# Fewer steps with a third product, and a weight's narrowing moved between two sums, in an FNet and gated-convolution kernel

## The chip, the cores and the metric

The kernel runs on one core of one Trainium2 chip. A core has TensorE (PE, the matrix engine; the profile lists its weight loads apart, as PEld), VectorE (DVE), ScalarE (ACT), GpSimd (POOL) and SyncE (SP), each with a queue of its own that runs in order. They meet through semaphores, on-chip memory (SBUF) and the eight banks of PSUM, into which TensorE writes. The metric is the time of the whole program on the device, in microseconds (us).

## The reference

Two layers follow each other. The first takes the real part of a Fourier transform over the sequence and the features; the second is a feed-forward layer whose gate is a convolution of length three over the sequence:

```python
# x: (8, 3136, 256) float32
x = np.fft.fft(np.fft.fft(x, axis=1), axis=2).real
h = np.maximum(x @ w_in, 0.0)                    # w_in: (256, 1024)
hp = np.pad(h, ((0, 0), (1, 1), (0, 0)))
conv = sum(conv_w[k] * hp[:, k:k + 3136] for k in range(3))   # conv_w: (3, 1024)
out = (h * (1.0 / (1.0 + np.exp(-conv)))) @ w_out             # w_out: (1024, 256)
```

All of it is float32. The weights `w_in`, `conv_w` and `w_out` come in as float64 and are read as pairs of 32-bit words.

## The kernel before

**Transform over the sequence.** For each batch the input is folded (`fold_ops`: 14 VectorE operations or pairs of them, about 1.2 us each) and then multiplied with tables of cosines and sines on TensorE, in nine "units" for the first batch and eight for the others. A unit has matmuls into a PSUM bank, for some a ScalarE copy, and a `fin`, two VectorE operations that write sums and differences. The results are two tables for a batch, `PQ[b][0]` (named `pt`) and `PQ[b][1]` (named `qt`), the cosine part and the sine part. The units for even frequencies k are `even_even` and `even`, those for odd k `odd_even` and `odd`. They use the symmetry of the transform: the frequencies k and S - k share both parts and differ only in the sign of one.

**Second layer.** The transform over the features is multiplied into `w_in` beforehand (`blocks`, `column`, giving `G` and `ge`). The main loop has 256 steps: 8 batches, 4 chunks of frequencies, 8 blocks of 128 hidden features. Step s passes through a pipeline of four cycles. In cycle t of the loop:

- `products(t + 1)`: on TensorE, `pb` is G1 times `qt`, and `pa` (seeded beforehand by ScalarE) gets G0 times `pt` added. The hidden values are relu(pa + pb) for the front rows and relu(pa - pb) for the mirrored back rows.
- `copies(t + 1)`: ScalarE copies `pb` into SBUF (`nb`), once with scale 1 for the front and once with scale -1 for the back.
- `combine(t)`: VectorE makes the two halves of `h`, each by a saturating add of `pa` and `nb` (L719).
- `seed(t + 2)` and `first_tap(t)` on ScalarE, `tap(t - 1, 1)` and `tap(t - 1, 2)` on VectorE (L730): the convolution, into `g`.
- `sigmoid(t - 2)` on ScalarE, `gate(t - 2)`: the product with `h`, shared between GpSimd (L753) and VectorE (L754).
- `mm2(t - 3)`: TensorE multiplies `g` into `w_out`, six or seven output tiles, summed over eight steps.

Side work is hung onto cycles in a table `side`, under (cycle, place): places are "first", "act", "dve", "pool", "load" and "pe". The folds of the next batch but one go to "dve", the units' matmuls of the next batch to "pe", their copies to "act" and their `fin` to "dve". VectorE's place "dve" lies between the two taps.

**The third product.** In some steps (`triple(s)`, which asks `third(i)`) TensorE adds G1 times `qt` to `pa` as well. Then `pa` holds the front half whole, ScalarE writes its relu (L705) instead of the copy for the front, and scales the copy for the back by -2 (L703). VectorE has one add less in `combine`. In the same cycles the gate is shared otherwise (`shares`): GpSimd takes a quarter of the columns instead of half, VectorE three quarters. `third(i)` holds for steps from 3 to `ends[2]` (44) that have side work in "dve" and none in "pe".

**The start.** A weight is made float32 by integer operations on its 32-bit words (`narrow`): a first part `power` (L543, L547, L548) and a second part `product` (L551, L557, L558, L561), seven VectorE operations for a quarter of `w_in`. `Weight.parts` returns the two as functions; `Weight.narrow` runs both at once. Near the end of the start, the units `us[4], us[2], us[3], us[7], us[8]` run in this order: the unit of the middle feature (its `fin` on GpSimd), then `even_even(1)`, `even(1)`, `even_even(0)`, `even(0)`. The second quarter, `w_in[1]`, is narrowed ahead of them (L821). It is used by `column(1)` and `blocks(1)` later. After the units come `column(0)` and `blocks(0)`, which take their PSUM banks from the same pool of four (`spare`) as the units.

Of the kernel before, what the change touches and what calls it, by code (L numbers as in the profile page):

```python
# [36 lines left out]
def kernel(  # L37
# [199 lines left out]
    def mend_row(par, half):  # L237

        for st in range(2):
            row = tabs[par][96:NP, st, HQ - 1]  # L240
            act(row, row, AF.Copy, scale=half[96:NP])
# [239 lines left out]
    def spread(b, cs):  # L481

        for c in cs:
            ch = chunks[c]
            eb[b, c] = ebp.tile([P, HN], F32, name="eb", tag="eb")[:, 0:ch.k1 - ch.k0]
            nc.sync.dma_start(out=eb[b, c], in_=ed[b:b + 1, ch.k0:ch.k1].to_broadcast([P, ch.k1 - ch.k0]))
# [121 lines left out]
    def raw_in(i):  # L608
        def f(sh):
            if i % 2 == 0:  # L610
                raws[i // 2] = wp.tile([P, 2, *sh[1:]], I32, name="raw", tag="w%d" % (i // 2))
            return raws[i // 2][:, i % 2]
        return f

    w_in = [Weight(w4[i], moe_w_in[:, i * N4:(i + 1) * N4].rearrange("(t p) n -> p t n", p=P), raw_in(i))
            for i in range(4)]
# [57 lines left out]
    def triple(s):  # L674

        return third(steps.index(s))

    def third(i):

        return 3 <= i < ends[2] and (i, "dve") in side and (i, "pe") not in side  # L680

    def row_of(s):
        hs[s] = hp.tile([P, HW], F32, name="h", tag="h")
# [48 lines left out]
    def shares(s):  # L732


        ch = chunks[s[1]]
        w = ch.w - 2
        n = ch.rest[0] if ch.last else w
        m = n - n // (4 if third(steps.index(s) + 2) else 2)
        return slice(0, m), slice(m, n), slice(n, w)
# [78 lines left out]
                                   lambda sh: xp.tile(sh, I32, name="raw", tag="xh"))  # L818
                    w_out.load(nc.sync)
    mend_row(0, half)  # L820
    w_in[1].narrow(0, 2)  # L821
    for i, u in enumerate(us[j] for j in (4, 2, 3, 7, 8)):
        u.matmuls(0, 1)
        u.copy()
        u.fin()
        if i == 0:
            flip()
            store()
            spread(0, range(1, len(chunks)))
# [13 lines left out]
    side = {}  # L843
# [23 lines left out]
    ends = [9, 20, per + 12] + [per * (b - 1) - 3 + max(11 - 4 * (b - 2), 0) for b in range(3, B)]  # L867
# [163 lines left out]
```

## Time and profile before

| | |
|---|---|
| time, median of 3 runs | 1192.77 us (1191.79 to 1192.78) |
| span of the profiled execution | 1191.0 us |
| TensorE busy | 1166.1 us (98%) |
| VectorE busy | 1128.6 us (95%) |
| ScalarE busy | 888.2 us (75%) |
| GpSimd busy | 408.9 us (34%) |
| records of pa<-qt, the third product | 44, 18.0 us |

A float32 product of the program appears as two matmul records, so the 44 records are 22 products. Matmuls are pipelined: the distance from one start to the next is what a matmul costs, and it is less than its record's length. The same holds for VectorE, where an operation's record (0.55 us for an add) is a little longer than the distance to the next (0.47 us). In an order of time each line shows the start, the length, the engine, the line of the code, the operation, what it writes and reads, and how many are merged; a bracket gives the idle time ahead of it and what ended it. L92 is the line of the helper that issues all matmuls.

### The profile page before, as it was taken

What the parts mean: (1) busy time and instruction counts of PE and PEld (TensorE: products, weight loads), DVE (VectorE), ACT (ScalarE), POOL (GpSimd) and SP (SyncE); (2) the same over time, 40 slices, a digit from 0 to 9 for tenths busy, and PEclk for the clock granted to TensorE, in tenths of its full rate; (3) what the DMA queues carried; (4) which work ended last, traced back from release to release, by engine and by line L of the source; (5) the groups of instructions that cost most, each with busy time, mean ns of one, the idle gap of its engine ahead of it and who ended that gap; (6) DMA issues with size and microseconds to landing.
All of it is one profiled execution on the core that took longest, in us unless ns stands there. A gap on an engine that the chain in (4) does not pass through costs nothing.

```text
span 1191.0 us, 15384 instructions
## 1 busy us (share of the span) xinstructions
PE 1166.1 (98%) x4846; PEld 897.9 (75%) x4846; DVE 1128.6 (95%) x1620; ACT 888.2 (75%) x1888; POOL 408.9 (34%) x476
## 2 busy tenths in 40 slices
PE   4999999999999999999999999999999999999998
PEld 2667777777777777777777777777777777777776
DVE  7899999899999999999998999999998998999996
ACT  2578667777678777877777777877786777888885
POOL 5226343423334333333333243432322232222222
PEclk9899999999999999999999999999999999999999
DMA  9803233121122121202121010310010100110001
GB/s 229 191 8 110 53 57 88 49 62 47 40 69 79 34 72 57 63 26 74 34 88 52 28 54 27 102 34 27 27 34 21 32 28 27 47 34 27 28 27 31
DMA packets 70068, 66.08 MB, mean 55 GB/s; under 512 B 28107, under 2 KB 57683, under 8 KB 69987
## 3 DMA queue, kind: packets, MB, share of 16 engines
q1 hardware_dynamic: 64349, 51.98, 15.6%
q0 software_dynamic: 5120, 12.85, 3.7%
q8 instruction: 38, 0.62, 0.2%
q14 instruction: 43, 0.35, 0.1%
q10 hardware_dynamic: 518, 0.28, 0.1%
HBM read 39.33 MB, written 25.74 MB: 55 GB/s over the span
## 4 chain that ended last, share of the span: by engine, by line
PE 93%; DVE 3%; ACT 1%; POOL 1%; issue 1%; DMA 0%; SPq 0%; POOLq 0%; ACTq 0%; DVEq 0%
PE po L92 56%; PE pa L92 15%; PE pb L92 14%; PE pd L92 8%; DVE g L730 1%; POOL xh L131 1%; DVE g L754 0%; DVE h L719 0%; DVE wout L551 0%; ACT os L778 0%; DVE raw L558 0%; ACT nb L708 0%; ACT g L725 0%; DMA out_dram<-os 0%; DVE wout L561 0%
## 5 line engine op out<-in xcount | busy, mean ns | idle before, releaser
L92 PE MATMUL po<-wout,g 128*128 128x256 f32 x3072 | 705.2, 379 | 2.7 <-DVE g L754 2.7
L92 PEld LDWEIGHTS po<-wout,g 128*128 128x128 f32 x3072 | 581.5, 189 | 144.7 <-issue 19.7
L730 DVE SCALAR_TENSOR_TENSOR g<-h,cw,g 128x770 f32<-128x770 f32 (+1 forms) x512 | 576.6, 1126 | 7.5 <-ACT g L725 3.9
L753 POOL TENSOR_TENSOR g<-g,h 128x385 f32<-128x385 f32 (+3 forms) x256 | 273.0, 1067 | 717.5 <-ACT g L745 555.7
L708 ACT ACTIVATE nb<-pb 128x386 f32<-128x386 f32 (+2 forms) x468 | 208.6, 500 | 172.5 <-PE pb L92 171.7
L745 ACT ACTIVATE g<-g 128x385 f32<-128x385 f32 (+5 forms) x512 | 244.6, 531 | 67.6 <-DVE g L730 64.2
L719 DVE CUSTOM_DVE_ANT_0 h<-pa,nb 128x386 f32<-128x386 f32 (+3 forms) x490 | 253.9, 556 | 6.4 <-POOL h L686 4.2
L725 ACT ACTIVATE g<-h,cw 128x770 f32<-128x770 f32 (+1 forms) x256 | 244.0, 953 | 0.0
L92 PE MATMUL pb<-qt,G 127*128 127x387 f32 (+2 forms) x512 | 214.3, 499 | 0.9 <-ACT G L641 0.9
L92 PE MATMUL pa<-pt,G 128*128 128x387 f32 (+2 forms) x512 | 211.8, 494 | 0.0
L672 ACT ACTIVATE pa<-eb,ge 128x387 f32<-128x387 f32 (+2 forms) x256 | 155.1, 606 | 0.6 <-ACT ft L477 0.6
L92 PEld LDWEIGHTS pa<-pt,G 128*128 128x128 f32 x512 | 97.1, 190 | 73.8 <-issue 18.4
L754 DVE TENSOR_TENSOR g<-g,h 128x385 f32<-128x385 f32 (+3 forms) x256 | 150.3, 587 | 2.4 <-ACT g L745 2.4
L92 PE MATMUL pd<-tab,w 98*128 98x196 f32 (+3 forms) x448 | 115.9, 356 | 0.0
L92 PEld LDWEIGHTS pb<-qt,G 127*128 127x128 f32 x512 | 91.7, 191 | 18.9 <-ACT G L641 2.0
L131 POOL DMA_INDIRECT xh<-in_x_dram,idx x64 | 99.7, 1558 | 13.0 <-issue 10.5
L92 PEld LDWEIGHTS pd<-tab,w 98*128 98x128 f32 (+1 forms) x448 | 82.7, 191 | 12.6
L778 ACT COPY os<-po 128x256 f32<-128x256 f32 x196 | 57.6, 396 | 6.6 <-PE po L92 3.3
L156 DVE TENSOR_TENSOR xh<-xh 98x1020 f32<-98x1020 f32 (+1 forms) x32 | 40.7, 1276 | 2.6 <-DMA xh<-in_x_dram,idx 2.5
L167 DVE TENSOR_TENSOR xh<-xh 98x1024 f32<-98x1024 f32 (+1 forms) x32 | 40.5, 1267 | 0.1
L178 POOL COPY w<-xh 98x4 f32<-98x4 f32 (+1 forms) x32 | 22.9, 716 | 6.1 <-DVE xh L167 3.6
L193 DVE TENSOR_TENSOR w<-xh 98x508 f32<-98x508 f32 (+1 forms) x32 | 23.5, 733 | 0.1
(124 smaller groups left out, 359.5 us busy)
## 6 DMA issues: line engine op xcount, KB each, us to landing
out_dram<-os SPq DMA_DIRECT2D x192, 128.0 KB
xh<-in_x_dram SPq DMA_DIRECT2D x16, 784.0 KB
eb<-ed SPq DMA_DIRECT2D x16, 193.5 KB
tab<-dft_seq_dram SPq DMA_DIRECT2D x4, 589.5 KB
raw<-in_moe_w_in_dram SPq DMA_DIRECT2D x4, 512.0 KB
raw<-in_moe_w_out_dram SPq DMA_DIRECT2D x1, 2048.0 KB
eb<-ed SPq DMA_DIRECT2D x8, 209.0 KB
eb<-ed SPq DMA_DIRECT2D x7, 193.0 KB
```

The source lines that it names most:

```text
L92: nc.tensor.matmul(o, l, r, start=start, stop=stop, skip_group_check=True)
L131: nc.gpsimd.indirect_dma_start(out=xh[b, h][0:NP, 7 - m].rearrange("p q d -> p (q d)"), out_offset=None, in_=bass.AP(tensor=x.tensor, offs ...
L156: vt(a[:, :, :, 1:D], a[:, :, :, 1:D], r[:, :, :, D - 1:0:-1], op=ALU.add)
L672: act(pa[s][:, 0:n], eb[b, c], AF.Copy, scale=ge[:, f:f + 1])
L708: act(nb[s][:, i, cols], p[:, cols], AF.Copy, scale=-1.0 if i else 1.0)
L719: nc.vector._custom_dve(TENSOR_ADD_SAT, out=to, in0=a[:, cols], in1=c[:, i, cols], s0=BIG, s1=0.0)
L725: act(gs[s], hs[s][:, 0:n], AF.Copy, scale=cw[:, 0, s[2]:s[2] + 1])
L730: stt(out=g, in0=h[:, k:k + n], scalar=cw[:, k, f:f + 1], in1=g, op0=ALU.mult, op1=ALU.add)
L745: act(gs[s][:, c], gs[s][:, c], AF.Sigmoid)
L753: gt(g[:, p], g[:, p], h[:, p], op=ALU.mult)
L754: vt(g[:, v], g[:, v], h[:, v], op=ALU.mult)
L778: nc.scalar.copy(out=osb[:, j % 2], in_=pt[:, j % 2])
```

## The change

There are two edits, and neither changes what is computed.

```diff
     def third(i):
-        return 3 <= i < ends[2] and (i, "dve") in side and (i, "pe") not in side
+        return 3 <= i < 12 and (i, "dve") in side
```

The third product is kept in steps 3 to 11 only. It relieves VectorE at the price of TensorE; the edit is meant to give TensorE its time back in the steps after 11.

```diff
     mend_row(0, half)
-    w_in[1].narrow(0, 2)
+
+    second = w_in[1].parts(0, 2)
     for i, u in enumerate(us[j] for j in (4, 2, 3, 7, 8)):
         u.matmuls(0, 1)
         u.copy()
+        for f in second[i - 1:i]:
+            f()
         u.fin()
         if i == 0:
             flip()
```

The slice is empty for i = 0, holds `power` for i = 1 and `product` for i = 2, and is empty again after that. So `power` now runs on VectorE ahead of the `fin` of `even_even(1)`, and `product` behind it and ahead of the `fin` of `even(1)`. It is meant to let VectorE finish the first of these sums earlier.

## The prediction

> **What bounds the kernel now.** I read the chain of waits first, then the stretches of the middle of the run, then the orders of time of TensorE and VectorE there, then those of the start.
>
> ```profile
> PE 93%; DVE 3%; ACT 1%; POOL 1%; issue 1%; DMA 0%; SPq 0%; POOLq 0%; ACTq 0%; DVEq 0%
> ```
> The chain of what ended last is 93% TensorE (PE), so in most of the run each microsecond of matmul is a microsecond of span. The busy shares (PE 98%, VectorE (DVE) 95%) warn that VectorE is close behind. By stretch (columns: length; busy of PE, weight load, DVE, ACT, POOL; granted clock; DMA):
> ```profile
> 107.00:120.00 13.00, 13.00 (x57) 9.79 (x56) 12.84 (x18) 10.69 (x31) 7.92 (x7) 1.00 0.36 105
> 185.00:257.00 72.00, 72.00 (x295) 53.78 (x294) 66.78 (x90) 54.12 (x115) 24.91 (x34) 1.00 0.18 54
> 257.00:330.00 73.00, 73.00 (x310) 56.59 (x309) 71.03 (x106) 52.73 (x112) 28.33 (x26) 1.00 0.19 58
> ```
> 107 to 140 us holds steps 12 to 17, 185 to 257 us steps 29 to 43. PE never idles there; VectorE has 5.2 us left of 72. Two cycles of PE, the first with the third product (pa<-qt), the second without:
> ```profile
> 236.51 0.81 PE L92 MATMUL pb<-qt,G 127*128 127x387 f32 x2
> 237.16 0.81 PE L92 MATMUL pa<-pt,G 128*128 128x387 f32 x2
> 237.81 0.82 PE L92 MATMUL pa<-qt,G 127*128 127x387 f32 x2
> 238.47 2.75 PE L92 MATMUL po<-wout,g 128*128 128x256 f32 x12
> 241.06 0.82 PE L92 MATMUL pb<-qt,G 127*128 127x387 f32 x2
> 241.71 0.82 PE L92 MATMUL pa<-pt,G 128*128 128x387 f32 x2
> 242.37 2.75 PE L92 MATMUL po<-wout,g 128*128 128x256 f32 x12
> ```
> From start to start, a product takes 0.65 us (237.81 to 238.47), a cycle 4.55 us with the third and 3.90 us without. VectorE's cycle of step 40, which has the third product:
> ```profile
> 240.62 0.55 DVE L719 CUSTOM_DVE_ANT_0 h<-pa,nb 128x386 f32<-128x386 f32 x1
> 241.09 1.13 DVE L730 SCALAR_TENSOR_TENSOR g<-h,cw,g 128x770 f32<-128x770 f32 x1
> 242.14 0.68 DVE L171 TENSOR_TENSOR xh<-xh 99x512 f32<-99x512 f32 x1
> 242.74 0.68 DVE L172 TENSOR_TENSOR xh<-xh 99x512 f32<-99x512 f32 x1
> 243.34 1.01 DVE L730 SCALAR_TENSOR_TENSOR g<-h,cw,g 128x770 f32<-128x770 f32 x1
> 244.28 0.75 DVE L754 TENSOR_TENSOR g<-g,h 128x578 f32<-128x578 f32 x1
> 245.19 1.03 DVE L719 CUSTOM_DVE_ANT_0 h<-pa,nb 128x386 f32<-128x386 f32 x2 [0.17 <-DVE g L754]
> ```
> One saturating add, two taps of 0.93, a fold of 1.2 us, a gate of 0.67: 4.4 us against PE's 4.55. Without the third product it will be two adds and a smaller gate against 3.90: VectorE becomes the longer of the two in every such step. That is the question of this change.
>
> The start, where the second edit lies (VectorE, then PE):
> ```profile
> 39.74 0.69 DVE L561 SCALAR_TENSOR_TENSOR win<-raw,win 128x512 f32<-128x512 f32 x1
> 40.35 0.35 DVE L298 TENSOR_TENSOR as<-as,po 128x197 f32<-128x197 f32 x1
> 40.62 0.35 DVE L300 TENSOR_TENSOR as<-po,as 128x196 f32<-128x196 f32 x1
> ```
> ```profile
> 41.07 1.67 PE L92 MATMUL po<-dm,win 128*128 128x1 f32 x8 [0.82 <-ACT eb L835]
> ```
> The narrowing (seven operations from 35.44 us, ending with L561) stands ahead of the sums L298 and L300, although their input was copied by ScalarE at 37.37. L300 releases the PSUM bank that column(0) takes, and PE idles 0.82 us until 41.07; the view names a ScalarE copy done at 40.78, but L300, ending at 40.97, fits better.
>
> **What the Trainium skill says.** "SBUF — State Buffer", section "SBUF: two separate sides": VectorE operations with two SBUF inputs and GpSimd operations that read SBUF contend for one port pair, held for a whole instruction. The trace agrees: the tap's shortest record is 1.00 us, and the one that meets a GpSimd gate at 257.73 takes 1.48. "GPSIMD Engine Reference", section "4.1 Engine selection": two-input elementwise work is about twice as slow on GpSimd; here 385 columns take 0.87 us against VectorE's 0.55. "TensorE: Matmul & The Clock Gate", section "What's actually happening": the array runs at half clock after an idle window of about 3.4 us and needs a busy one to return. Here the granted clock is 0.99 in 37.9 to 41.3 us, 0.50 in 41.3 to 48.1, and 1.00 after, which fits two such windows.
>
> **First edit: which steps.** A step has the third product now if it is in 3 to 43, has VectorE side work and no PE side work. By the schedule in the code these are 3 to 13, 15, 17, 29, 30, 32, 34, 35, 37, 38, 40 and 42: 22 steps, which matches the 44 records of pa<-qt. After the change 3 to 11 remain. All nine have it already, so dropping the PE condition changes nothing. Thirteen steps lose it.
>
> Per step lost: **PE** -0.65 us (-0.71 for the 418 columns of steps 29 and 30). **ScalarE** two copies before, two after (L703 and L705 0.49 each, L708 0.50 each): nothing. **VectorE** +0.47 for the second add (start to start: two take 0.94, one 0.47); the gate falls from three quarters to half of 770 columns, 0.67 to 0.47, so -0.20; net +0.27. **GpSimd** gate 192 to 385 columns, 0.52 to 0.87 us, +0.35, hidden as such (busy 25 of 72 us), but it can block VectorE. Bounds of that block: 0 (the operations don't meet) and 0.35 a step (all exposed). The tap means of the stretches, 1.076 us where nine of sixteen steps have the quarter share and 1.087 where none has, nearly coincide, so I take 0.05.
>
> The output products of step s wait for VectorE's gate of s, which ends where its adds of step s+3 begin. Hence a ledger of both engines.
>
> Steps 12 to 18, VectorE in one piece from 107.08: its cycles 4.19, 4.70, 4.50, 4.0, 4.42, 4.19, 4.41 become, with +0.27 in 12, 13, 15 and 17, ends of 111.5, 116.5, 121.0, 125.3, 129.7, 134.2, 138.6. PE, 0.65 less in four cycles, would reach its output products earlier than these ends allow and waits 0.4, 0.6 and 1.1 us in cycles 12 to 14. Of 2.6 us saved 0.75 are left at cycle 18. With the contention I take **0.5**. VectorE is then 0.9 us late, but steps 19 to 28 carry matmuls of the next batch on PE (46 us of PE against 44 of VectorE without its waits), so it catches up and the 0.5 stays.
>
> Steps 28 to 42: VectorE takes from 184.70 to 253.12, 68.42 us, of which 5.07 idle by its brackets (0.89, 0.17, 0.20, 0.25, 0.45, 0.92, 1.76, 0.26, 0.17), so 63.35 of work; +9 x 0.32 gives 66.2. PE goes from 185.07 to 253.41, 68.34; less 7 x 0.65 and 2 x 0.71 it is 62.4. VectorE now sets the pace. Its end becomes 184.70 - 0.5 + 66.2 = 250.4, which is when the output products of cycle 43 can start, instead of 254.72: **4.3 earlier**, with the first 0.5 inside it. PE alone could have been there at 248.2. Its lead of 2.5 us over the need at step 28 is used up, so cycle 44, where VectorE takes 4.87 us (257.00 to 261.87) and PE 4.56, costs **0.3** back. After that PE has longer cycles (5.2 us) and the old state returns. Sum: -4.0.
>
> **Second edit.** The two halves of the narrowing (three and four operations) move behind the first and second unit of even k. No operation is added. The three end at 37.05, the sums wait for ScalarE's copy (37.37), end near 38.0; then the four (3.3 us before, partly stretched by GpSimd work up to 39.16, say 3.0) end near 41.1 and the second unit's sums near 42.1, as before. So nothing behind is delayed. Column(0) follows the matmul that ends at 40.25 without a gap, 0.8 earlier, and ends about 41.75. Blocks(0), which began at 42.55 behind it, then waits for the second unit's sums (42.1) and starts **0.4 to 0.5 earlier**; PE, ScalarE and then VectorE (idle 0.90 before its first adds) follow, so it carries through. I take -0.5.
>
> Together: 1192.8 - 4.0 - 0.5 = **1188.3**.
>
> **Rivals.**
> (1) VectorE binds in place of PE, as worked out: 1188.3. For it: 5.2 us of VectorE slack in 72, and its work a step. Chance 0.58.
> (2) The same, and the closed gap keeps the clock up: blocks(0) take 3.76 us at half clock, the same matmuls 1.89 at 51.03. With some of the next products about 2.2 saved: 1186.1. Against it: PE soon waits again for the second unit's sums. Chance 0.13.
> (3) VectorE's waits absorb everything and PE gets its full 11 x 0.65 + 2 x 0.71 = 8.6: 1183.7. Against it: the 66.2 above. Chance 0.05.
> (4) The whole 0.35 of longer GpSimd work lands on VectorE: 9 x 0.3 more is 2.7 in the second stretch, and the first gains nothing: about 1191.3. For it: the 1.48 us tap. Chance 0.16.
> (5) Slower: each larger GpSimd gate blocks VectorE for its whole 0.87 us. The second stretch then is 63.35 + 9 x 1.14 = 73.6, 5.2 above today, less the lead of 2.5, so +2.7; the first has no gain: about 1195.5. Against it: today's half-share steps lose about 0.07 us a tap. Chance 0.08.
>
> **How the numbers follow.** The forecast is (1). The range from 1185.6 to 1191.5 takes in (1), (2) and (4), 0.87 less some spread at its ends. The bound of 0.2% is 2.4 us, so faster is below 1190.4: (1) to (3) and a quarter of (4), 0.80; within the bound the rest of (4), 0.12; slower (5), 0.08.
>
> **What would show it.** Right: pa<-qt has 18 records and the adds 503; PE shows idle time released by VectorE's gate (L754) of about 2 us in steps 12 to 14 and about 2 in 28 to 45; VectorE loses its 5 us of idle time there; column(0) starts near 40.3. Wrong: PE without idle time (rival 3), taps clearly longer than 1.09 us (4, 5), or waits of VectorE for GpSimd's memsets or ScalarE's copies in 29 to 42, which I count as gone.

## The result, and the profile after

The changed kernel takes 1187.98 us (median; 1186.53 to 1190.16) against 1192.61 us before: ratio 0.9964, 95% interval 0.9947 to 0.9981, so 4.6 us faster. A second set of runs gave 1186.52 us against 1192.41, ratio 0.9959 (0.9946 to 0.9973). The forecast was 1188.3 us.

The chain of what ended last, in the profile after:

```profile
PE 89%; DVE 7%; issue 1%; POOL 1%; ACT 1%; DMA 0%; DVEq 0%; SPq 0%; POOLq 0%; ACTq 0%
PE po L92 54%; PE pb L92 14%; PE pa L92 13%; PE pd L92 8%; DVE g L730 3%; DVE h L719 1%; DVE g L754 1%; POOL xh L131 1%; DVE raw L558 0%; DVE xh L167 0%; DVE wout L551 0%; ACT os L778 0%; DVE w L194 0%; DVE win L551 0%; DMA out_dram<-os 0%
```

VectorE's share of the chain has gone from 3% to 7%. The stretches that match those shown of before (same columns):

```profile
106.00:119.00 13.00, 12.15 (x51) 8.96 (x52) 13.00 (x20) 10.54 (x32) 5.79 (x7) 1.00 0.33 94
181.00:252.00 71.00, 70.40 (x293) 52.92 (x291) 70.25 (x104) 56.14 (x120) 26.25 (x35) 1.00 0.21 60
252.00:325.00 73.00, 73.00 (x311) 56.90 (x310) 71.16 (x105) 53.02 (x112) 29.40 (x27) 1.00 0.19 59
```

In the first VectorE is busy all the time and TensorE is not; in the second both are near full, 70.4 and 70.25 of 71 us; the third, behind the change, is as before. TensorE in the two cycles whose match was shown of before:

```profile
230.81 0.81 PE L92 MATMUL pb<-qt,G 127*128 127x387 f32 x2
231.47 0.82 PE L92 MATMUL pa<-pt,G 128*128 128x387 f32 x2
232.52 2.86 PE L92 MATMUL po<-wout,g 128*128 128x256 f32 x12 [0.23 <-DVE g L754]
235.21 0.82 PE L92 MATMUL pb<-qt,G 127*128 127x387 f32 x2
235.87 0.81 PE L92 MATMUL pa<-pt,G 128*128 128x387 f32 x2
236.52 2.75 PE L92 MATMUL po<-wout,g 128*128 128x256 f32 x12
```

The product pa<-qt is gone, and its 0.65 us has become 0.23 us of waiting for VectorE's gate and a shorter cycle: 4.40 us instead of 4.55. VectorE's cycle of step 40:

```profile
235.77 1.02 DVE L719 CUSTOM_DVE_ANT_0 h<-pa,nb 128x386 f32<-128x386 f32 x2
236.71 1.05 DVE L730 SCALAR_TENSOR_TENSOR g<-h,cw,g 128x770 f32<-128x770 f32 x1
237.68 0.68 DVE L171 TENSOR_TENSOR xh<-xh 99x512 f32<-99x512 f32 x1
238.28 0.68 DVE L172 TENSOR_TENSOR xh<-xh 99x512 f32<-99x512 f32 x1
238.88 1.01 DVE L730 SCALAR_TENSOR_TENSOR g<-h,cw,g 128x770 f32<-128x770 f32 x1
239.81 0.55 DVE L754 TENSOR_TENSOR g<-g,h 128x385 f32<-128x385 f32 x1
```

Two adds and the smaller gate make 4.51 us, against 4.40 of work before, and the next adds follow without the bracket of 0.17 us that stood there.

To see where the time came from, take the start of the pb<-qt matmuls of each cycle in both profiles and subtract. The profile after is ahead by 0.94 us at cycle 0, still 0.94 at cycle 11, 1.84 at cycle 18, 1.72 at cycle 28, 6.40 at cycle 42, and 6.29 from cycle 45 to the end. So 0.8 us comes from steps 12 to 17 (0.9 won, 0.1 given back), 4.6 us from steps 29 to 42 (4.7 won, 0.1 given back), together **5.35**, and 0.94 us from the start. The profiled execution was the fastest of its set, 1186.53 us.

### The profile page after: what moved, and what is told of

It is laid out like the page before. It is cut to its first block, busy times and chain, and to the rows that moved or that the text cites. A ratio compares the mean times of both kernels' runs of the same rounds, so it can differ in the third digit from the quotient of the medians.

```text
span 1184.7 us, 15354 instructions
## 1 busy us (share of the span) xinstructions
PE 1158.7 (98%) x4820; PEld 891.6 (75%) x4820; DVE 1128.7 (95%) x1633; ACT 886.7 (75%) x1888; POOL 407.6 (34%) x476
## 4 chain that ended last, share of the span: by engine, by line
PE 89%; DVE 7%; issue 1%; POOL 1%; ACT 1%; DMA 0%; DVEq 0%; SPq 0%; POOLq 0%; ACTq 0%
PE po L92 54%; PE pb L92 14%; PE pa L92 13%; PE pd L92 8%; DVE g L730 3%; DVE h L719 1%; DVE g L754 1%; POOL xh L131 1%; DVE raw L558 0%; DVE xh L167 0%; DVE wout L551 0%; ACT os L778 0%; DVE w L194 0%; DVE win L551 0%; DMA out_dram<-os 0%
## 5 line engine op out<-in xcount | busy, mean ns | idle before, releaser
L753 POOL TENSOR_TENSOR g<-g,h 128x385 f32<-128x385 f32 (+2 forms) x256 | 270.4, 1057 | 721.1 <-ACT g L745 542.1
L708 ACT ACTIVATE nb<-pb 128x386 f32<-128x386 f32 (+2 forms) x494 | 219.9, 500 | 168.2 <-PE pb L92 167.5
L745 ACT ACTIVATE g<-g 128x385 f32<-128x385 f32 (+4 forms) x512 | 244.8, 531 | 81.8 <-DVE g L730 78.4
L719 DVE CUSTOM_DVE_ANT_0 h<-pa,nb 128x386 f32<-128x386 f32 (+2 forms) x503 | 260.0, 556 | 2.5 <-POOL h L686 2.5
L754 DVE TENSOR_TENSOR g<-g,h 128x385 f32<-128x385 f32 (+2 forms) x256 | 147.7, 577 | 2.4 <-ACT g L745 2.4
L193 DVE TENSOR_TENSOR w<-xh 98x508 f32<-98x508 f32 (+1 forms) x32 | 23.0, 720 | 0.1
```

The costliest lines, as they stand in the source:

```text
L708: act(nb[s][:, i, cols], p[:, cols], AF.Copy, scale=-1.0 if i else 1.0)
L719: nc.vector._custom_dve(TENSOR_ADD_SAT, out=to, in0=a[:, cols], in1=c[:, i, cols], s0=BIG, s1=0.0)
L745: act(gs[s][:, c], gs[s][:, c], AF.Sigmoid)
L753: gt(g[:, p], g[:, p], h[:, p], op=ALU.mult)
L754: vt(g[:, v], g[:, v], h[:, v], op=ALU.mult)
```

## The experiments

**The edits apart.** The first edit alone changes the line of `third` only:

```diff
-        return 3 <= i < ends[2] and (i, "dve") in side and (i, "pe") not in side
+        return 3 <= i < 12 and (i, "dve") in side
```

> The first edit alone: the third product in steps 3 to 11 only, the narrowing of the second quarter as before. Theory (VectorE sets the pace where the product is dropped, so TensorE keeps only part of its 8.6 us): 4.0 to 5.3 us faster than before, 1187.4 to 1188.7. Rival A (TensorE keeps all 8.6 us): 1184.1. Rival B (the longer GpSimd gate blocks VectorE, and the gain is mostly the second edit's): less than 2 us faster, above 1190.7. In the profile the theory wants VectorE without idle time and TensorE waiting for the VectorE gate in steps 12 to 14.

Measured: 1186.34 us against 1192.41, ratio 0.9955 (0.9942 to 0.9969). By cycles it is ahead by 0.89 us at cycle 0 and by 6.22 at cycle 45, that is 5.33 between, as in the kernel after. More than forecast, and less than the 8.6 us of TensorE work. It has the start's 0.9 us too, without the second edit.

The second edit alone keeps `third` as before and takes the new loop with `second`.

> The second edit alone: third products as before, the narrowing moved between the sums. Theory (TensorE's gap ahead of column(0) closes, the rest of the start follows by the same amount): 0.5 to 0.9 us faster than before, 1191.7 to 1192.1, and all steps earlier by one amount. Rival C (the closed gap keeps the clock up through blocks(0)): 2.2 us or more faster, 1190.4 or less, with blocks(0) near 1.9 us instead of 3.8. Rival D (the start is hidden behind VectorE's work up to step 9): no change, 1192.6.

Measured: 1192.20 us against 1192.41, ratio 1.0002 (0.9993 to 1.0010): nothing. The first edit is the whole gain. TensorE at the start of this run shows why column(0) didn't gain:

```profile
39.56 0.38 PE L92 MATMUL po<-dm,win 128*128 128x1 f32 x2
41.36 1.44 PE L92 MATMUL po<-dm,win 128*128 128x1 f32 x6 [1.42 <-DVE win L561]
```

Two of its eight records run at once, the other six wait for L561, the last operation of the narrowing of the *other* quarter. In the kernel after the same wait is 0.30 us.

**More runs of the kernels.** The kernel after, unchanged:

> The kernel after, unchanged, for more runs of it beside the others on one chip. Both theories: 1188.0 within its scatter so far (1186.5 to 1190.2). If the scatter comes from the start (arrival of transfers, granted clock), a second profile differs from the first before step 0 and agrees with it from step 12 on in the distances between steps.

Measured: 1186.52 us (1186.35 to 1187.44). By cycles it is ahead of before by 1.13 us at cycle 0 and by 6.48 at cycle 45: 5.35 between, as in its first profile. Only the start differs.

The kernel before, unchanged:

> The kernel before, unchanged, for a second profile of its start. If the 0.94 us by which the first profile of the kernel after is ahead at step 0 is the second edit's, this profile reaches the second products (cycle 0) near 49.6 us again. If it is scatter of the start (arrival of the row er, the phase of the clock's change), it lies anywhere from 48.5 to 50.8 us, as in the other profiles, while from cycle 0 on every distance is that of the first profile within 0.1 us.

Measured: 1192.11 us, ratio 0.9999 (0.9990 to 1.0007). This profile reaches cycle 0 at 48.65 us, 0.99 us ahead of the first profile of the same code, and ends 0.8 us earlier; of its distances after cycle 0 only one part differs, 0.2 us that it loses in cycles 19 to 23. So a lead like the 0.94 us at the start of the profile after comes without the second edit too: with the first edit alone (0.89), and with neither (0.99). It is scatter of the start, of which the last section shows one source.

**Why the second edit gives nothing.** Two quarters of `w_in` share a tile in which their columns alternate (the first and the second half of each row block). The next kernel is the kernel after with each quarter contiguous:

```diff
-    win = [... [:, 0:F].rearrange("p (t n) -> p t n", t=2)
+    win = [... [:, 0:F].rearrange("p (h t n) -> p h t n", h=2, t=2)
-    w4 = [win[i // 2][:, :, i % 2 * N4:(i % 2 + 1) * N4] for i in range(4)]
+    w4 = [win[i // 2][:, i % 2] for i in range(4)]
```

> The kernel after with the two quarters of w_in that share a tile laid out one after the other in it (each quarter contiguous), so that no instruction on one quarter spans the other. Theory: with interleaved quarters the matmuls of column(0) wait for the end of the narrowing of the other quarter (L561), which replaced the wait for the PSUM bank; with contiguous ones column(0) runs through at once behind the matmul of the row er, near 6.4 us after the start of the matmuls of ea, blocks(0) waits for the sums of the second unit alone, and the start is 0.3 to 0.5 us shorter from there to products of step 0. In the total 0 to 0.5 us faster than the kernel after. Rival: the wait for L561 is genuine (another semaphore of the same queue) and stays at 0.3 to 1.4 us.

Measured: 1188.43 us (1185.53 to 1190.45), ratio 0.9965 (0.9952 to 0.9977), no faster than the kernel after. Its profile is of the slowest of the six executions, 1190.45 us. The wait for L561 is gone: column(0) is one piece, and blocks(0) waits for L312, the sums of the second unit:

```profile
41.07 1.05 PE L92 MATMUL po<-dm,win 128*128 128x1 f32 x8
43.61 2.90 PE L92 MATMUL po<-win,dm 128*128 128x256 f32 x6 [1.49 <-DVE qt L312]
```

So the layout made the wait. But the sums themselves are late. ScalarE and VectorE of this run show what they wait for:

```profile
37.79 0.92 ACT L384 ACTIVATE er<-er 1x392 f32<-1x392 f32 x1 [0.85 <-DMA er<-qt]
38.73 0.58 ACT L294 COPY as<-po 128x197 f32<-128x197 f32 x2
```
```profile
39.09 0.36 DVE L298 TENSOR_TENSOR as<-as,po 128x197 f32<-128x197 f32 x1 [1.42 <-ACT as L294]
```

ScalarE's flip of the row `er` waits for a transfer, the copy L294 is queued behind it, and VectorE's first sums wait for that copy. In the kernel before, VectorE spends this time on the four operations of `product`; after the second edit it stands idle with `product` queued behind the waiting sums. Twelve of the profiles give a table (time from the start of the matmuls of `ea` to the start of blocks(0)):

| kernel | sums ahead of `product` | flip waits for `er`, us | `ea` to blocks(0), us |
|---|---|---|---|
| before, two profiles | no | 0; 1.22 | 8.85; 8.69 |
| first edit alone | no | 0.36 | 8.50 |
| after; no third product | yes | 0; 0 | 8.15; 8.16 |
| after again; drop in 29 to 42 | yes | 0.44; 0.51 | 8.60; 8.63 |
| drop in 12 to 17, two profiles | yes | 1.27; 0.78 | 9.37; 8.99 |
| second edit alone | yes | 1.15 | 9.53 |
| half share; quarter kept | yes | 1.48; 1.45 | 9.60; 9.83 |

In the three profiles without the second edit (8.50 to 8.85 us) the distance doesn't follow the transfer. With the edit it is 8.15 us when the row is in time, and 9.60 to 9.83 us when the row is 1.5 us late. What the edit wins in some executions it loses in others.

The last experiment on the start mends both: contiguous quarters, the flip behind the copies, and one ScalarE operation in place of two VectorE ones in the narrowing:

```diff
-    second = w_in[1].parts(0, 2)
+    second = w_in[1].parts(0, 2, room)
...
-        if i == 0:
+        if i == 3:
             flip()
```

> The kernel after with contiguous quarters of w_in, ScalarE instead of VectorE for two of the seven operations that narrow the second quarter, and the sign flip of the row er behind the ScalarE copies of the sums for even k instead of ahead of them. Theory H (VectorE sets the pace from the narrowing to step 9, and the sums of the first unit wait for a ScalarE copy queued behind the flip, which waits for a transfer): two operations of 0.46 us and up to 1.1 us of waiting less, 0.9 to 1.5 us faster than the kernel after. Rival (the start is bound by something else, a transfer or the matmuls at half clock): no change.

Measured: **1185.64 us** (1185.26 to 1186.80), ratio 0.9945 (0.9931 to 0.9958), the fastest of all. `ea` to blocks(0) is 7.49 us, and TensorE runs on through all of blocks(0) without a wait:

```profile
40.36 1.05 PE L92 MATMUL po<-dm,win 128*128 128x1 f32 x8
41.42 3.64 PE L92 MATMUL po<-win,dm 128*128 128x256 f32 x8
```

It is ahead of before by 1.90 us at cycle 0, 0.8 to 1.0 more than the two profiles of the kernel after, and by 7.24 at cycle 45. The median is 0.9 us below the second set of the kernel after, but the two weren't run side by side, and the intervals overlap. So a gain over the kernel after isn't shown by the medians. The three parts weren't run apart either.

**Does VectorE set the pace of steps 3 to 42?** First, no third product at all:

```diff
-        return 3 <= i < 12 and (i, "dve") in side
+        return False
```

> The kernel after, with no third product in any step. Theory (VectorE is the longer engine in steps with side work): nine more steps give VectorE 0.27 us each, so 2.4 us slower than the kernel after, about 1190.4, though TensorE is freed of another 5.9 us. Rival A (TensorE bounds): 5.9 us faster than the kernel after, about 1182. Rival B (only GpSimd's share matters): also slower, by 3 us or more, with taps clearly longer than 1.09 us.

Measured: 1189.66 us, ratio 0.9981 (0.9974 to 0.9988), 3.1 us slower than the kernel after beside it, although TensorE is freed of another 5.9 us. By distances it loses 1.8 us from cycle 0 to cycle 11, where the kernel after neither wins nor loses. Four of TensorE's waits there:

```profile
68.66 2.86 PE L92 MATMUL po<-wout,g 128*128 128x256 f32 x12 [1.83 <-DVE g L754]
79.04 2.86 PE L92 MATMUL po<-wout,g 128*128 128x256 f32 x12 [1.83 <-DVE g L754]
84.89 2.86 PE L92 MATMUL po<-wout,g 128*128 128x256 f32 x12 [1.68 <-DVE g L754]
90.88 2.86 PE L92 MATMUL po<-wout,g 128*128 128x256 f32 x12 [1.83 <-DVE g L754]
```

VectorE does set the pace there, so in steps 3 to 11 the third product pays for itself. Without it GpSimd takes half of the gate in these steps too. That share isn't the cause of the loss: between 60 and 105 us the taps are no longer than in the kernel after (1.016 us on average, against 1.020), so rival B falls.

Second, the kernel after with GpSimd's share of the gate left at a quarter in the 13 steps that lost the product:

```diff
-        m = n - n // (4 if third(steps.index(s) + 2) else 2)
+        m = n - n // (4 if quarter(steps.index(s) + 2) else 2)   # quarter: third() as it was before
```

> The kernel after, but GpSimd keeps a quarter of the gate in the 13 steps that lost the third product, as the kernel before had it there. Theory (VectorE's own work sets the pace there): each of these steps gives VectorE 0.20 us, 4 in the first stretch and 9 in the second, less what TensorE still has in hand: 1.5 to 2.6 us slower than the kernel after, 1188.2 to 1189.5 beside about 1186.8. Rival B (the meeting of VectorE and GpSimd is what costs): no slower than the kernel after, 1186.8 or less.

Measured: 1189.97 us, ratio 0.9982 (0.9975 to 0.9989), a smaller gain than that of the kernel after, as the theory has it. From cycle 0 to 45 its profile wins 2.70 us on before instead of 5.35. By cycles, the stretches of the edit account for half of these 2.65 us: 0.44 is missing in cycles 11 to 18 and 0.87 in cycles 28 to 45. That is 0.10 us for each of the 13 steps, and not the whole 0.20. The other 1.35 us is lost between cycles 18 and 28, where the edit changes no step, after GpSimd operations that are much longer than usual, among them the gate in cycle 17 (L757 in this kernel):

```profile
130.07 4.14 POOL L757 TENSOR_TENSOR g<-g,h 128x192 f32<-128x192 f32 x1
134.58 4.54 POOL L131 DMA_INDIRECT xh<-in_x_dram,idx  x1 [0.19 <-issue]
```

So VectorE's work costs time there, but at half the size that the total suggests. Whether the quarter share brings on the long operations isn't shown.

Third, GpSimd takes half in steps 3 to 11 as well, where the third product stays:

```diff
-        m = n - n // (4 if third(steps.index(s) + 2) else 2)
+        m = n - n // 2
```

> The kernel after, with GpSimd taking half of the gate in steps 3 to 11 as well (the third product stays there). Theory (VectorE sets the pace up to step 9: TensorE waited 0.5, 0.8 and 0.9 us for its gate): VectorE has 0.20 us less in each, so 1.0 to 1.5 us faster than the kernel after, near 1185.5, and these three waits shrink. Rival B (GpSimd, busy with gathers there, or its meeting with VectorE takes it back): no faster, or slower than the kernel after.

Measured: 1190.16 us, ratio 0.9984 (0.9978 to 0.9991): slower, rival B. Between 60 and 105 us the gate on VectorE falls from 6.57 to 4.95 us busy (nine each), but the taps rise from 18.84 to 20.45 (nineteen each): 1.62 less and 1.61 more. The reason is in the order of time. VectorE and GpSimd in this run:

```profile
97.72 0.55 DVE L719 CUSTOM_DVE_ANT_0 h<-pa,nb 128x386 f32<-128x386 f32 x1
98.19 1.47 DVE L730 SCALAR_TENSOR_TENSOR g<-h,cw,g 128x770 f32<-128x770 f32 x1
```
```profile
97.98 0.86 POOL L753 TENSOR_TENSOR g<-g,h 128x385 f32<-128x385 f32 x1 [1.25 <-ACT g L745]
```

and in the kernel after, in step 12, where the third product is dropped:

```profile
106.14 1.02 DVE L719 CUSTOM_DVE_ANT_0 h<-pa,nb 128x386 f32<-128x386 f32 x2
107.08 1.01 DVE L730 SCALAR_TENSOR_TENSOR g<-h,cw,g 128x770 f32<-128x770 f32 x1
```
```profile
106.25 0.86 POOL L753 TENSOR_TENSOR g<-g,h 128x385 f32<-128x385 f32 x1 [1.36 <-issue]
```

GpSimd's gate begins with the adds. An add reads one input from PSUM and isn't lengthened. A gate of 0.86 us that begins inside the single add reaches to 98.84, into the tap, which takes 1.47 us instead of 1.01. Behind two adds (0.94 us) the same gate is over, at 107.11, when the tap begins, at 107.08. So the half share fits the steps without a third product, and the quarter those with it. In steps 3 to 11 the longer taps take back what the half share gives. (Between 183 and 202 us of the kernel after the taps have 832 columns and the half share 448; that gate takes 0.98 us, reaches a little into the tap, and the tap grows by 0.13 to 0.15 us.) The larger part of this run's loss, 2.5 of 3.3 us by distances, falls in cycles 14 to 16 and comes with GpSimd operations of 4.3 and 4.4 us (see the end).

**The two stretches apart.** The drop in steps 12 to 17 only:

```diff
-        return 3 <= i < 12 and (i, "dve") in side
+        return (3 <= i < 12 or 18 <= i < ends[2]) and (i, "dve") in side and (i, "pe") not in side
```

> Both edits, but the third product is dropped in steps 12 to 17 only and kept in the nine steps from 29 to 42. Theory: the first stretch is worth 0.8 to 0.9 us (TensorE saves 2.6 and waits for the rest), so 1191.6 to 1191.8 beside 1192.4 of before, and the second stretch the 4.6 us that are left. Rival A (TensorE keeps all): 1189.8. Rival E (nothing is won in the first stretch, because the VectorE lag is carried into the second): 1192.4.

Measured: 1193.25 us against 1192.25, ratio 1.0012 (1.0005 to 1.0019): no gain, the theory's 1191.7 is missed. Yet its profile, of an execution of 1191.37 us, wins 0.78 us from cycle 0 to 45. The same kernel a second time:

> The kernel with the drop in steps 12 to 17 alone, a second time, for another profile of it. Theory F: 1191.7, and 0.8 us won from step 11 to 18 that stay. Theory G: near 1193, with a profile in which what was won up to step 18 is lost between steps 19 and 23, where TensorE waits for VectorE behind a long GpSimd gate or gather.

Measured: 1192.81 us, ratio 1.0003 (0.9995 to 1.0012). The profile again wins 0.9 us from cycle 11 to 18 and 0.74 up to cycle 45, and nothing is lost between 19 and 23; theory G's picture doesn't show. This execution (1193.60 us) is late at the start, 0.73 us behind before at cycle 0, and 0.8 us late behind the last products. The drop in steps 29 to 42 only:

```diff
-        return 3 <= i < 12 and (i, "dve") in side
+        return 3 <= i < 18 and (i, "dve") in side and (i, "pe") not in side
```

> Both edits, but the third product is dropped in the nine steps from 29 to 42 only and kept in 12, 13, 15 and 17. Theory F (each stretch stands for itself, as the distances between steps in the profiles say: 0.9 and 4.6 us): 1187.8 beside 1192.4 of before. Theory G (the VectorE lag that is left behind by the drop in 12 to 17 costs it back in most executions, as the median of the run with that stretch alone suggests): 1186.3 or less, faster than the kernel after.

Measured: 1188.26 us against 1192.08, ratio 0.9965 (0.9952 to 0.9979), not 1186.3 or less, so theory G falls. Its profile wins 4.6 us from cycle 28 to 45, as forecast by F. By distances the two stretches add up (0.8 and 4.6); by medians they are -1.0 and 3.8 and don't add up to the 6.1 of the first edit. What the unprofiled executions of the drop in 12 to 17 lose stays open. Long GpSimd operations cost 1.4 to 2.5 us in the profiles of three other kernels, so they are a candidate, but no profile of this kernel shows that loss.

## Why the prediction was right, and where it was not

- **The mechanism of the first edit held.** VectorE became the pace-maker of the steps that lost the product, and TensorE kept part of its 8.6 us. VectorE's idle time between steps 28 and 43 fell from 5.07 to 0.58 us, pa<-qt has 18 records and the adds 503, all as stated. The 0.58 us that are left are a wait for GpSimd's memset (L686), which I had counted as gone.
- **Its size was too small: -4.0 against -5.35.** The mis-sized term is the growth of VectorE's work. Between the adds of steps 28 and 43 VectorE takes 65.44 us (182.74 to 248.18), 0.58 idle, so 64.86 of work; forecast 66.2. Nine steps at +0.32 should have added 2.9 us, and they added about 1.5. Both parts of the term were too large. The second adds and the smaller gates cost 2.05 us from start to start, 0.23 a step instead of 0.27. And the meeting of GpSimd and VectorE, for which I had added 0.05 a step, gave back about 0.3 us in all. The taps did lose 0.8 us more to it than before, but three folds (L193) that ran beside GpSimd operations and were 0.33 to 0.45 us longer than elsewhere have their usual 0.68 us now. That they fall clear is timing that I didn't foresee, so in part it is luck. The two tap means from which I took the 0.05 mix two shapes: by shape they are 1.076 and 1.058 us for 770 columns, and 1.076 and 1.239 us for 832 columns, so they don't coincide. This stretch won 4.7 instead of 3.8, the first 0.8 instead of 0.5, and cycle 44 gave back 0.1 instead of 0.3.
- **TensorE's waits in cycles 12 to 14** were forecast as 0.4, 0.6 and 1.1 us and are 0.34, 0.30 and 0.28. VectorE's cycle 13 had 4.70 us before, with a tap and a fold stretched by GpSimd (1.18 and 1.53 us); I carried that on as 4.97, and it is 4.45. In 28 to 45 it waits 0.6 us, not about 2: there the two engines came out even.
- **The second edit failed: -0.5 forecast, none measured.** The step that failed is "Column(0) follows the matmul that ends at 40.25 without a gap". The wait for the PSUM bank was replaced by one for L561, and VectorE's sums took on ScalarE's wait for the row. I had read the ScalarE copy's end in one profile (37.37) as fixed, without asking what stands ahead of it in its queue.
- **The total of 1188.3 was met by 0.3 us**, partly because the errors, 1.35 too little and 0.5 too much, have opposite signs; the second set, 1186.52, shows the difference.
- **The rivals.** TensorE keeping all (3) fell with the runs without any third product. (4) and (5), GpSimd taking it back, didn't happen in the sum over the steps of the change, but (4)'s mechanism is real: it took the whole gain of the half share in steps 3 to 11. (2) didn't happen: the granted clock is 0.57 in 42 to 46 us of the profile after. "SBUF — State Buffer" in the Trainium skill, section "SBUF: two separate sides", is borne out in its detail too: beside a gate on GpSimd the tap with two SBUF inputs is lengthened (1.47 us), the add with one is not (0.55 us).

## What to carry to other kernels

Where two engines are both above 93% busy, an edit that moves work from one to the other is worth about the slack of the other (here 4.7 us, where VectorE had 5.07 us idle); keep a ledger of both through each stretch, and count collisions by when an operation falls, not by how long it is. When work is moved from ahead of a wait to behind it, look at what the awaited engine has in its queue: work that stood in front may have been hiding a transfer. And two parts of a tile that alternate in memory can be made to wait for each other although no byte is shared.

## What the runs showed of the hardware that was not expected

**Long gates on GpSimd.** GpSimd's gate of 385 columns takes 0.9 us or less in 143 of 183 cases of the profile after, but every one of the fourteen profiles has five to seven gates of more than 2 us. One of 4.95 us, in the kernel with contiguous quarters, is followed by a slow gather, a second slow one and a long tap on VectorE (1.01 us elsewhere). GpSimd, then VectorE during the long gate, then VectorE and TensorE behind it:

```profile
126.04 4.95 POOL L753 TENSOR_TENSOR g<-g,h 128x385 f32<-128x385 f32 x1 [1.53 <-ACT g L745]
131.18 4.43 POOL L131 DMA_INDIRECT xh<-in_x_dram,idx  x1 [0.18 <-PE pb L92]
135.64 0.88 POOL L753 TENSOR_TENSOR g<-g,h 128x385 f32<-128x385 f32 x1
136.45 0.94 POOL L178 COPY w<-xh 99x4 f32<-99x4 f32 x1
137.34 0.10 POOL L180 MEMSET w<- 99x4 f32 x1
137.62 3.16 POOL L131 DMA_INDIRECT xh<-in_x_dram,idx  x1 [0.19 <-issue]
140.81 1.70 POOL L753 TENSOR_TENSOR g<-g,h 128x385 f32<-128x385 f32 x2
```
```profile
126.72 1.01 DVE L730 SCALAR_TENSOR_TENSOR g<-h,cw,g 128x770 f32<-128x770 f32 x1
127.65 1.21 DVE L167 TENSOR_TENSOR xh<-xh 99x1024 f32<-99x1024 f32 x1
128.78 1.01 DVE L730 SCALAR_TENSOR_TENSOR g<-h,cw,g 128x770 f32<-128x770 f32 x1
129.71 0.55 DVE L754 TENSOR_TENSOR g<-g,h 128x385 f32<-128x385 f32 x1
130.18 1.02 DVE L719 CUSTOM_DVE_ANT_0 h<-pa,nb 128x386 f32<-128x386 f32 x2
```
```profile
140.74 2.60 DVE L730 SCALAR_TENSOR_TENSOR g<-h,cw,g 128x770 f32<-128x770 f32 x1
```
```profile
144.02 2.21 PE L92 MATMUL pd<-tab,w 98*128 98x392 f32 x6 [0.66 <-DVE as L330]
```

The long gate lasts through a row of VectorE operations that each read two inputs from SBUF, and it ends at 130.99, 0.81 us after VectorE's next adds begin. By these times GpSimd is the one that waits here, for nearly a whole cycle of VectorE. In the profile after, four of the five gates of more than 2 us end 0.80 or 0.81 us after an add begins as well. Why the tap waits in one case (97.98 us of the half-share run) and the gate in another isn't shown.

The five long gates of the profile after cost nothing: TensorE waits for nothing in their neighbourhood. The execution with contiguous quarters lost 1.9 us between cycles 19 and 23, where the kernel after lost 0.1. The kernel with the quarter share kept lost 1.5 us in the same cycles (4.14 us for the gate, 4.54 for the gather), and the half-share run, at 102.60 us, shows the same sequence (4.33, 4.43, 0.87). In all three a tap of 2.6 us follows. Why it comes in these executions and not in others isn't shown.

**The clock at the start.** Between 40 and 44 us the granted clock falls from full to half in each of the fourteen profiles, for 3.4 us in eight and for 6.8 us in six. The stretch ahead of the fall and the half-clock stretch, first before, then after (columns as above):

```profile
37.90:41.30 3.40, 2.58 (x13) 1.74 (x13) 3.20 (x7) 0.81 (x2) 2.91 (x4) 0.99 1.01 369
41.30:48.10 6.80, 6.34 (x18) 4.64 (x18) 6.46 (x14) 1.90 (x5) 2.85 (x7) 0.50 0.67 206
```
```profile
38.90:42.30 3.40, 3.00 (x16) 2.03 (x14) 3.30 (x7) 0.58 (x3) 2.76 (x3) 1.00 1.00 370
42.30:45.70 3.40, 3.29 (x8) 2.52 (x8) 3.19 (x8) 0.47 (x2) 2.23 (x6) 0.51 1.00 285
```

TensorE is recorded as busy for 2.58 and 3.00 of the 3.40 us ahead of the fall. The idle window that the prediction cites for it doesn't show; the lengths of one and two windows do. From the start of blocks(0) to cycle 0 it takes 6.0 to 6.3 us where the clock is down for 3.4 us, and 6.4 to 7.3 where it is down for 6.8. This is one source of the scatter at the start. No edit decides it alone: with the same code of the start, the first edit alone has 3.4 us and the two profiles of before have 6.8, and the profiles with the second edit have both. Whether the second edit changes how often the short one comes, fourteen profiles are too few to tell.
